# Two half loads of one row each in place of one load of two rows, for the gate rows of a head pair

## The chip, the cores and the metric

The kernel runs on one core of a Trainium2 chip. The metric is the device time of one execution in microseconds. Lower is better.

## The reference

The computation has three stages, all in float32, on 2 x 576 = 1152 tokens.

1. Causal attention with a forget gate, 2 batches x 8 heads, 576 positions, head size 64. `cum` is the running sum of log f along the positions:

```
scores = q @ k.T / 8
decay  = cum[:, None] - cum[None, :]
attn   = softmax(where(causal, scores + decay, -1e9))
x      = attn @ v            # heads side by side: 1152 x 512
```

2. A mixture of four experts, each weighted by a normalised probability p: `x = sum_e p[:, e] * (relu(x @ w1[e]) @ w2[e])`, with 512 x 1024 and 1024 x 512 weights.
3. A last block `out = (g(x @ w_in)) @ w_out` with g(h) = h * sigmoid(1.702 h) and 2048 hidden units.

Within a row of the softmax the term `cum[row]` is constant and falls out, so the kernel needs only a row vector for every head, `-cum[column]`, the same for all query rows. These vectors are the gate rows of the change.

## The kernel before, in words

Every matrix product of the experts is done as three products of rounded float32 parts (high x high, low x high, high x low), so each weight tile passes through a split: ScalarE or POOL writes the high part `whi` (lines 53 and 56), VectorE the low part `wlo` (line 173). Raw weights arrive by SP's queue in `wst`, four buffers; `load_pair` issues the next load when the split of an earlier one is done.

The attention runs while the first expert blocks are computed. `attention()` is a generator over units (one query tile of a head pair, or two tiles of one head). Each step emits stages of several units: the scores on TensorE (line 436), the maximum on VectorE (line 464), the exponential on ScalarE (line 480), the division by the sum on POOL (line 491), the transposes on TensorE (line 510), the copies `ph` on ScalarE, and the product with the values on TensorE (line 540). The main loop pulls steps of this generator between groups of expert matmuls (lines 639 and 683).

For each head pair of the later passes (eight in all) `load_heads` brings keys and queries (`kq`, `qr`), `prep_parts` and `prep_queries` split them on POOL (`khi`, `klo`, `qhi`, `qlo`), and `load_cum` brings the gate rows from the small DRAM tensor `cumd` (16 rows, one per head, 576 columns). It issues a tile `cb` for each of the two heads, one row broadcast to 128 partitions, and a tile `cbs` of 128 x 576 in which the first 64 partitions hold the row of the first head and the other 64 that of the second. `cbs` serves the last query tile, which has only 64 rows per head, so both heads share one 128-row tile. `prep_cum` then adds the causal triangle on POOL: to `cb` in lines 391 and 394, to the last 64 columns of `cbs` in line 397, once for each half. VectorE reads `cbs` in line 464. There are two `cbs` buffers.

All these loads are issued by `load` (line 62) on SP's queue, which works through its instructions in order; an instruction that must wait holds up all behind it. Tiles carry their dependences, and a planner that simulates the run (`schedule_with_timeline_sim`) writes down the order of each engine's instructions. Only the start (`start[0]`, `keep_in_program_order`) and a few steps (`pinned`) are fixed by hand. When the attention is done, `begin_late` frees its memory and `mlp_convert` starts to convert the last block's weights on VectorE (lines 222 to 238).

Of the kernel before, what the change touches and what calls it, by code (L numbers as in the profile page):

```python
# [15 lines left out]
B, H, S, D = 2, 8, 576, 64  # L16
# [19 lines left out]
def attn_moe_mlp(ctx: ExitStack, tc: tile.TileContext, qk0, qk1, qk2, v0, vp, fg, dp, wa_moe, wb_moe, wa_mlp, wb_mlp, outT):  # L36
# [8 lines left out]
    def pool(name, bufs, space=None, scope=ctx):  # L45
        kw = {} if space is None else {"space": space}
        return scope.enter_context(tc.tile_pool(name=name, bufs=bufs, **kw))
# [12 lines left out]
    def load(out, in_):  # L60

        ins = nc.sync.dma_start(out=out, in_=in_)
        if start[0]:
            tc.keep_in_program_order(ins)
# [37 lines left out]
    cumd = pool("cumd", 1, bass.MemoryType.DRAM).tile([16, S], F32, name="cumd")  # L102
# [271 lines left out]
    def load_cum(p, h0):  # L374

        cs, b, s0 = p
        st = pairs[p, h0]
        r = b * H + h0
        st["cb"] = [cb_p.tile([128, 896], F32, tag="cb", name="cb") for _ in range(2)]
        for g, cb in enumerate(st["cb"]):  # L380
            load(cb[:, :512], cumd[r + g:r + g + 1, :512].to_broadcast([128, 512]))
        st["cbs"] = cbs_p.tile([128, S], F32, tag="cbs", name="cbs")
        load(st["cbs"], cumd[r:r + 2, :].unsqueeze(1).to_broadcast([2, 64, S]))

    def prep_cum(p, h0):

# [172 lines left out]
    def attention():  # L559
# [21 lines left out]
        for i in range(len(seq) + L_X2 + 1):  # L581
# [3 lines left out]
            if i == 0:  # L585
                load_cum(*nxt[0])
# [3 lines left out]
            def prepare():  # L590
                for k in new:
                    prep_parts(*k)
                for k in new_q:
                    prep_queries(*k)
                for k in new:
                    load_cum(*k)
                    prep_cum(*k)
# [297 lines left out]
```

## Time and profile before

| what | value |
|---|---|
| time, median of 3 runs | 735.25 us (733.9 to 736.05) |
| the profiled execution | 733.54 us |
| its span, first to last instruction | 731.8 us |
| TensorE matmuls busy | 711.1 us, 97% |
| VectorE, POOL, ScalarE busy | 460.5, 291.0, 267.9 us |
| mean granted TensorE clock | 0.991 |
| moved by DMA | 68.83 MB, mean 94 GB/s |

All times inside the trace are microseconds from the start of the span. The time of an execution is a little longer than its span. Busy shares are averages over stages: the attention fills the first 225 us, the rest is expert and last-block matmuls.

### The profile page before, as it was taken

Reading aid. Unit: us, or ns where it says so; the run is one execution under the profiler, and the core shown is the slowest. Engines: PE = TensorE matmul, PEld = TensorE weight load, DVE = VectorE, ACT = ScalarE, POOL = GpSimd, SP = SyncE. Lnnn points to the kernel's source line nnn. Section 1 sums busy time; section 2 is a strip of 40 time slices with the busy share of each in tenths; the row PEclk is TensorE's granted clock in tenths of the full one; section 3 lists DMA queues with packets and bytes.
Section 4 is the critical chain, followed back from the end, with each engine's and each line's share of the span. In section 5 each row is a group of like instructions: output and inputs, shape, how many; then the busy total and the mean of one; then the engine's idle time right before and its main releaser. Section 6 shows DMA issues by size and latency. Waiting matters only on the chain.

```text
span 731.8 us, 12044 instructions
## 1 busy us (share of the span) xinstructions
PE 711.1 (97%) x4519; PEld 682.8 (93%) x4519; DVE 460.5 (63%) x1029; ACT 267.9 (37%) x630; POOL 291.0 (40%) x371
## 2 busy tenths in 40 slices
PE   7987989999999999999999999999999999999998
PEld 3776878898899999999998999999999999999997
DVE  5575737677758999999999542345962124424422
ACT  5354745576632233222221221223354433333320
POOL 6589787765422022332232432232462222222220
PEclk9899999999999999999999999999999999999999
DMA  8786643432225465453343210000100000000012
GB/s 261 226 251 219 175 159 127 134 101 67 81 88 195 144 203 161 144 189 116 115 144 116 87 30 29 1 1 1 58 1 0 1 1 1 1 1 0 1 44 87
DMA packets 31226, 68.83 MB, mean 94 GB/s; under 512 B 3224, under 2 KB 4768, under 8 KB 31168
## 3 DMA queue, kind: packets, MB, share of 16 engines
q1 hardware_dynamic: 31128, 68.02, 29.1%
q8 instruction: 36, 0.59, 0.3%
q14 instruction: 22, 0.18, 0.1%
q10 hardware_dynamic: 40, 0.04, 0.0%
HBM read 65.62 MB, written 2.41 MB: 93 GB/s over the span
## 4 chain that ended last, share of the span: by engine, by line
PE 69%; DVE 14%; DMA 6%; POOL 5%; issue 3%; ACT 1%; SPq 1%; DVEq 0%; ACTq 0%; POOLq 0%
PE m L683 32%; PE m L639 30%; PE s L436 3%; PE x L540 3%; DVE wlo L173 3%; DMA wst<-in_wa_moe_dram 2%; PE t L510 2%; DMA cbs<-cumd 2%; POOL e L491 2%; DVE cvd L236 1%; DVE hl L666 1%; DVE tmp L697 1%; DVE wf L230 1%; DVE cvt L224 1%; DMA mst<-in_wb_mlp_dram 1%
## 5 line engine op out<-in xcount | busy, mean ns | idle before, releaser
L699 POOL TENSOR_TENSOR acc<-acc,tmp 128x384 f32<-128x384 f32 (+3 forms) x112 | 111.7, 1009 | 237.3 <-DVE tmp L697 235.3
L683 PE MATMUL m<-hh,whi 128*128 128x384 f32 (+2 forms) x640 | 129.3, 321 | 0.2 <-DVE acc L694 0.2
L683 PE MATMUL m<-hh,wlo 128*128 128x384 f32 (+2 forms) x640 | 127.7, 320 | 1.2 <-DVE wlo L173 1.2
L683 PE MATMUL m<-hl,whi 128*128 128x384 f32 (+2 forms) x640 | 128.0, 319 | 0.0
L639 PE MATMUL m<-xh,wlo 128*128 128x384 f32 (+2 forms) x624 | 126.3, 320 | 0.0
L639 PE MATMUL m<-xl,whi 128*128 128x384 f32 (+2 forms) x624 | 126.2, 321 | 0.0
L639 PE MATMUL m<-xh,whi 128*128 128x384 f32 (+2 forms) x624 | 125.6, 321 | 0.0
L56 ACT ACTIVATE whi<-wst 128x512 fp32r<-128x512 f32 x104 | 65.3, 632 | 128.9 <-PE m L639 69.0
L173 DVE TENSOR_TENSOR wlo<-wst,whi 128x512 fp32r<-128x512 f32 x112 | 92.7, 830 | 24.6 <-ACT whi L56 18.2
L683 PEld LDWEIGHTS m<-hh,wlo 128*128 128x128 f32 x640 | 106.2, 189 | 1.9 <-DVE wlo L173 1.9
L683 PEld LDWEIGHTS m<-hh,whi 128*128 128x128 f32 x640 | 106.8, 190 | 0.6 <-DVE acc L694 0.4
L683 PEld LDWEIGHTS m<-hl,whi 128*128 128x128 f32 x640 | 106.4, 188 | 0.2
L639 PEld LDWEIGHTS m<-xh,wlo 128*128 128x128 f32 x624 | 104.1, 188 | 0.2
L639 PEld LDWEIGHTS m<-xl,whi 128*128 128x128 f32 x624 | 104.0, 188 | 0.2
L639 PEld LDWEIGHTS m<-xh,whi 128*128 128x128 f32 x624 | 103.7, 188 | 0.2
L674 POOL TENSOR_TENSOR hl<-tmp,hh 128x384 fp32r<-128x384 f32 x48 | 49.1, 1025 | 133.2 <-ACT hh L56 133.2
L665 ACT ACTIVATE hh<-m 128x384 fp32r<-128x384 f32 (+2 forms) x112 | 49.0, 437 | 114.4 <-PE m L639 114.0
L666 DVE SCALAR_TENSOR_TENSOR hl<-m,hh 128x384 fp32r<-128x384 f32 (+2 forms) x112 | 54.8, 492 | 32.5 <-ACT hh L665 32.5
L697 DVE TENSOR_TENSOR tmp<-m,dpb 128x384 f32<-128x384 f32 (+2 forms) x80 | 40.9, 512 | 33.3 <-PE m L683 26.8
L672 DVE TENSOR_TENSOR tmp<-m,sg 128x384 f32<-128x384 f32 x48 | 26.6, 554 | 54.5 <-ACT sg L671 52.7
L491 POOL TENSOR_SCALAR e<-e,sm 128x128 f32<-128x128 f32 (+4 forms) x72 | 46.5, 657 | 25.4 <-DVE sm L489 17.2
L480 ACT ACTIVATE e<-e,mx 128x128 f32<-128x128 f32 (+4 forms) x72 | 42.0, 583 | 33.3 <-DVE mx L464 29.2
(96 smaller groups left out, 774.8 us busy)
## 6 DMA issues: line engine op xcount, KB each, us to landing
wst<-in_wa_moe_dram SPq DMA_DIRECT2D x28, 512.0 KB, 3.7
wst<-in_wb_moe_dram SPq DMA_DIRECT2D x28, 512.0 KB, 3.8
mst<-in_wa_mlp_dram SPq DMA_DIRECT2D x16, 512.0 KB, 3.9
mst<-in_wb_mlp_dram SPq DMA_DIRECT2D x16, 512.0 KB, 3.7
cb<-cumd SPq DMA_DIRECT2D x16, 256.0 KB, 8.0
qr<-in_qk_dram SPq DMA_DIRECT2D x12, 256.0 KB, 9.4
kq<-in_qk_dram SPq DMA_DIRECT2D x8, 352.0 KB, 2.9
vd<-in_vp_dram SPq DMA_DIRECT2D x8, 320.0 KB, 8.2
```

Source lines behind the costliest of these rows:

```text
L56: return nc.scalar.activation(out=out, in_=in_, func=AF.Copy)
L173: sub = nc.vector.tensor_sub(lf, raw, f(hf))
L480: nc.scalar.activation(out=e[:, off:off + w], in_=e[:, off:off + w], func=AF.Exp, scale=-1.0, bias=mx, accum_out=sm[:, 0, k:k + 1])
L491: last_norm[:] = [nc.gpsimd.tensor_scalar(out=e[:, off:off + w], in0=e[:, off:off + w], scalar1=sm[:, 0, i:i + 1], scalar2=1.0, op0=ALU.mu ...
L639: nc.tensor.matmul(p[:, :n], lhsT=w[:, k, :], rhs=x[c][:, k, :], start=(j == 0 and k == 0), stop=(j == 2 and k == 3))
L665: nc.scalar.activation(out=hh[:, g, :n], in_=p[:, :n], func=AF.Relu)
L666: nc.vector.scalar_tensor_tensor(out=hl[:, g, :n], in0=p[:, :n], scalar=0.0, in1=f(hh[:, g, :n]), op0=ALU.max, op1=ALU.subtract)
L672: nc.vector.tensor_mul(t[:, :n], p[:, :n], s[:, :n])
L674: nc.gpsimd.tensor_sub(hl[:, g, :n], t[:, :n], f(hh[:, g, :n]))
L683: nc.tensor.matmul(p[:, :n], lhsT=w[:, k, :], rhs=x[:, k, :n], start=(j == 0 and k == 0), stop=(j == 2 and k == 3))
L697: nc.vector.tensor_mul(t[:, :n], p[:, :n], d)
L699: nc.gpsimd.tensor_add(a, a, t[:, z])
```

## The change

```diff
@@ -380,7 +380,8 @@
         for g, cb in enumerate(st["cb"]):
             load(cb[:, :512], cumd[r + g:r + g + 1, :512].to_broadcast([128, 512]))
         st["cbs"] = cbs_p.tile([128, S], F32, tag="cbs", name="cbs")
-        load(st["cbs"], cumd[r:r + 2, :].unsqueeze(1).to_broadcast([2, 64, S]))
+        for g in range(2):
+            load(st["cbs"][64 * g:64 * g + 64], cumd[r + g:r + g + 1, :].to_broadcast([64, S]))
 
     def prep_cum(p, h0):
 
```

Before, one load takes two rows of `cumd`, each repeated 64 times (a source of 2 x 64 x 576), and writes the 128 partitions of `cbs`. After, there are two loads: each takes one row, repeated 64 times, and writes 64 partitions. The bytes and the tile are the same.

## Rows read from the trace of the kernel before

**Rows 1.** Timeline of TensorE: start, us, what, idle time before it and releaser.
```profile
63.95 3.81 PE L540 MATMUL x<-ph,vd 128*64 128x320 f32 x16 [4.52 <-ACT ph L56]
...
92.36 0.65 PE L510 MATMUL t<-identr,e 128*128 128x128 f32 x4 [2.09 <-POOL e L491]
99.53 0.55 PE L510 MATMUL t<-identr,e 128*128 128x128 f32 x3 [0.78 <-POOL e L491]
105.09 0.66 PE L510 MATMUL t<-identr,e 128*128 128x128 f32 x4 [1.07 <-POOL e L491]
```

**Rows 2.** Busy time by stretch: length, PE, PEld, DVE, ACT, POOL, clock, DMA, GB/s.
```profile
63.95:67.10 3.15, 3.15 (x12) 2.78 (x14) 1.67 (x6) 2.64 (x9) 3.08 (x8) 0.51 0.35 111
```

**Rows 3.** Chain of waits, 30 to 85 us: start, us, what; the DMA pieces.
```profile
33.34 12.34 DMA cbs<-cumd
...
50.43 11.70 DMA wst<-in_wa_moe_dram
...
77.69 3.74 DMA cb<-cumd
```

**Rows 4.** Timeline of ScalarE around 62 us.
```profile
62.24 0.63 ACT L56 ACTIVATE whi<-wst 128x512 fp32r<-128x512 f32 x1 [4.78 <-DMA wst<-in_wa_moe_dram]
```

**Rows 5.** Timeline of VectorE around 49 us.
```profile
49.44 0.88 DVE L173 TENSOR_TENSOR wlo<-wst,whi 128x512 fp32r<-128x512 f32 x1 [1.56 <-POOL whi L53]
```

**Rows 6.** Timeline of POOL, 45 to 95 us.
```profile
45.75 0.70 POOL L397 TENSOR_TENSOR cbs<-cbs,tri 64x64 f32<-64x64 f32 x2 [3.25 <-DMA cbs<-cumd]
...
78.62 1.20 POOL L397 TENSOR_TENSOR cbs<-cbs,tri 64x64 f32<-64x64 f32 x2 [5.17 <-DMA cbs<-cumd]
79.89 1.71 POOL L363 TENSOR_TENSOR klo<-kq,khi 128x704 fp32r<-128x704 f32 x1
...
88.54 0.77 POOL L53 TENSOR_SCALAR khi<-kq 128x704 fp32r<-128x704 f32 x1
89.29 1.43 POOL L391 TENSOR_TENSOR cb<-cb,tri 128x384 f32<-128x384 f32 x1
...
94.61 0.71 POOL L397 TENSOR_TENSOR cbs<-cbs,tri 64x64 f32<-64x64 f32 x2 [2.30 <-DMA cbs<-cumd]
```

**Rows 7.** Waits over the run: who for whom, us in total, times, longest.
```profile
POOL cbs L397 <- DMA cbs<-cumd: 16.2, 6, 5.2
```

**Rows 8.** Waits of SP's queue over the run.
```profile
SPq L62 <- DMA cbs<-cumd: 5.9, 1, 5.9
...
SPq L202 <- PE t L510: 1.8, 1, 1.8
```

**Rows 9.** Timeline of SP's queue: issues of cbs loads.
```profile
70.18 0.51 SPq L62 DMA_DIRECT2D cbs<-cumd  x1
...
83.17 0.51 SPq L62 DMA_DIRECT2D cbs<-cumd  x1
```

**Rows 10.** Busy time by stretch, columns as in Rows 2.
```profile
75.00:76.00 1.00, 1.00 (x9) 0.96 (x9) 0.64 (x2) 1.00 (x4) 0.00 (x0) 1.00 0.13 51
78.00:79.00 1.00, 1.00 (x11) 1.00 (x10) 1.00 (x3) 1.00 (x3) 0.38 (x1) 1.00 1.01 391
```

**Rows 11.** DMA issues: count, KB each, median us from issue to landing.
```profile
wst<-in_wa_moe_dram SPq DMA_DIRECT2D x28, 512.0 KB, 3.7
...
kq<-in_qk_dram SPq DMA_DIRECT2D x8, 352.0 KB, 2.9
...
dpb<-dpT SPq DMA_DIRECT2D x2, 288.0 KB, 8.9
```

**Rows 12.** Issue durations on SP, ns min/median/max, first and last start (by tile).
```profile
L62 SPq DMA_DIRECT2D cbs<-cumd x8: 500/506/575, 14.1 to 154.9; - x8
...
L62 SPq DMA_DIRECT2D cb<-cumd x16: 326/360/976, 12.2 to 151.2; - x16
```

**Rows 13.** Busy time by stretch, columns as in Rows 2.
```profile
15.00:20.00 5.00, 3.99 (x12) 1.96 (x13) 4.02 (x17) 3.55 (x13) 1.36 (x2) 0.59 1.08 354
...
340.00:350.00 10.00, 10.00 (x60) 10.00 (x59) 10.00 (x19) 1.26 (x3) 3.75 (x3) 1.00 0.51 159
```

## The prediction

> **What bounds the kernel now.** I first read the busy table of the page: TensorE (PE) is busy for 711.1 of 731.8 us, so a change that touches no PE work can win only what PE loses to waits and to a low clock. The next view is the waits of PE in the order of time. After 64 us PE has four waits above 0.3 us: 4.52 us ahead of the value matmuls at 63.95 us, released by ScalarE, and 2.09, 0.78 and 1.07 us ahead of transposes between 92 and 106 us, all three released by POOL's normalisation of line 491 [rows 1]. From there to the end PE hardly waits, so a microsecond won in these places should reach the end. The first wait has a tail: from 63.95 to 67.10 us, just after PE stood idle, the granted clock is 0.51, the lower of the two levels (1.2 GHz), which costs 3.15 x 0.49 = 1.5 us [rows 2].
>
> Then I ask what ends last before these places. The chain of waits runs through three loads: the gate rows `cbs`, 12.34 us from 33.34 us on; a weight load `wst`, 11.70 us from 50.43 us on; and a `cb` load, 3.74 us [rows 3]. The weight load is the one behind the 4.52 us: ScalarE stands still for 4.78 us in front of the split of these weights at 62.24 us, and the copy that the value matmuls need is queued behind that split [rows 4]. It was issued late too, because VectorE's split, which frees the buffer, waited 1.56 us for POOL [rows 5], and POOL had stood still for 3.25 us before the `cbs` addition at 45.75 us. POOL does the same again for 5.17 us before 78.62 us and 2.30 us before 94.61 us [rows 6]; over the run it waits 16.2 us for these loads, in 6 places [rows 7]. SP also stands still for 5.9 us because of a `cbs` load [rows 8]. In the order of its issues that is the eighth load after the one of 33.34 us, which had to land first.
>
> Why is a load of 288 KB so slow? The SP queue issues two of them at 70.18 and 83.17 us [rows 9]; POOL sees them land at 78.62 and 94.61 us, after 8.4 and 11.4 us. While the first runs alone, at 75 to 76 us, the mean busy share of the 16 DMA engines is 0.13 at 51 GB/s; a `cb` load of 256 KB, a row broadcast to 128 partitions, brings the share to 1.01 and 391 GB/s at 78 to 79 us [rows 10]. 0.13 x 16 is 2.1: the transfer with two rows runs on two engines, one for each row, and the broadcast of one row on all of them. At 51 GB/s its 294,912 bytes alone take 5.8 us. Anything issued behind it (part of every load that is spread over 16 engines) waits on those two engines, which is the second reason for the 11.70 us of the weight load.
>
> **The change, part by part.** It removes eight loads that occupy two engines each and adds sixteen of 147,456 bytes, each with 64 as its first dimension; no compute instruction changes.
>
> *The new landing time.* The trace has no broadcast to 64 partitions. The nearest row is the `cb` load in the chain, with 3.74 us [rows 3]; the shortest of a like size is `kq` (352 KB) with 2.9 us and the longest the broadcast `dpb` (288 KB, in a crowded stretch) with 8.9 us [rows 11]. I take 3.7 us for a pair of halves and keep 2.9 and 8.9 as ends. With 3.7 us the load issued at 70.18 lands at 73.9; POOL was ready at 78.62 - 5.17 = 73.45, so 4.7 of its 5.17 us go. For the load of 83.17 all 2.30 go. The load of 33.34 may take 9.1 us before POOL (ready at 42.50) notices, more than the 8.9 of the worst row: all 3.25 go. So POOL is 3.25 us earlier by 46 us, 7.9 by 79 and 10.2 by 95.
>
> *The wait of 4.52 us and its clock.* ScalarE was ready for the weights at 62.24 - 4.78 = 57.46 us. With POOL 3.25 us earlier the weight load is issued at 47.2 instead of 50.43; with the typical 3.7 us of such a load [rows 11] it lands at 50.9, with its present 11.70 at 58.9, which would leave 1.4 us of the wait. Two blocked engines fewer speak for the first. I take the whole wait and its clock: 4.52 + 1.5 = 6.0 us (ends: 0 if the weights come late for another reason, 6.0).
>
> *What is late next.* Between 64 and 73 us POOL is only 3.25 us earlier while PE would be 6.0: PE can meet POOL's normalisations there and give back between 0 and 2.8 us. I take the middle, 1.4.
>
> *The waits for POOL at 92 to 106 us* sum to 3.94 us. POOL gains 10.2 us by then, PE 4.6, so POOL could cover all of it; but its inputs come from VectorE and ScalarE, which follow PE and get only PE's part. Ends 0 and 3.9; I take 2.0.
>
> *The added issues.* A `cbs` issue takes 506 ns on SP, a `cb` issue, the nearest for a half, 360 ns [rows 12]: 8 x (2 x 0.36 - 0.51) = 1.7 us more on SP in all, and one load more per head pair in a sequence in which the eighth load behind another waits for it. SP's own waits hide it. Without that cover it would be at most 0.2 us per pair on the load's way, 1.7 us in all.
>
> *The other waits on cbs* (16.2 - 3.25 - 5.17 - 2.30 = 5.5 us in three more places) have PE busy beside them; I count them at nothing, with 0.5 us as the upper end.
>
> Sum: 6.0 - 1.4 + 2.0 - 0 = 6.6 us. The profiled execution took 733.54 us (span 731.8), so 726.9 for its like. It was 1.7 us below the median of 735.25 us; against that median the forecast is 728.6 us. The terms' ends give from about 1 us slower (first term 0, issues 1.7, 0.5 won) to 10.4 us faster.
>
> One rule speaks against the change. The Trainium skill, page "DMA: Bandwidth & Descriptors", section "Rules for kernel authors", advises not to cut a transfer into two disjoint partition halves, since both halves use the same 16 engines and serialise. By that rule the time would stay at 735. The trace agrees only with half of its premise: the broadcast of one row does fill 16 engines (share 1.01), the one transfer that is cut here does not (0.13) [rows 10].
>
> **The rivals.**
> *Given back where VectorE is full.* From 230 to 400 us VectorE converts the later weights and is busy 10.00 of 10 us in a stretch such as 340 to 350 [rows 13]. If that work does not start earlier, PE arrives early and waits, and the time is 735.2. For it: the full VectorE. Against it: the load that starts the conversion is let go by PE's last transposes (SP waits 1.8 us for them) [rows 8], so it moves with PE.
> *The halves don't spread, or they serialise.* Then the loads stay near 8 us and nothing moves: 735. Against it stands the `cb` row at share 1.01; for it only that no load to 64 partitions is in the trace.
> *Slower: a new written order.* The order of every engine's instructions comes from a planner that simulates the loads. With two loads in place of one it can put a pair's preparation on POOL (klo 1.71, khi 0.77, cb 1.43 and what belongs to them, at least 3.9 us [rows 6]) ahead of a normalisation that PE's transposes wait for, between 80 and 106 us, where PE already follows POOL. Each pair placed so costs PE 3.9 us. One leaves 2.7 us of the gain; two cost 7.8 and turn it to 1.2 us slower, 736.5. So two pairs is the point from which it decides. For it: the order is not pinned in this stretch. Against it: the same data dependences and about the same bytes.
> *More than forecast.* If POOL's lead covers all of 3.94 us and PE gives nothing back, 9.9 us go; if the stretch at 15 to 20 us, where PE is busy 3.99 of 5 us at a clock of 0.59 [rows 13], also profits because the first `cbs` load no longer holds two engines, up to 13: 722 to 725.
>
> **How the numbers follow.** Forecast (2.3 to 9 us faster) 0.66; more than that 0.08; given back 0.09; no spreading 0.05; new order or another new wait with a loss 0.12. Below 0.3% (2.2 us), about what a measurement of this kernel tells from no change, lie the two neutral rivals: same 0.14. Faster 0.74, slower 0.12. The likeliest case alone spans 726 to 733. The range goes from 722, the larger gain, to 736.5, where the slower rival begins to win.
>
> **What would show it.** Right: the landing of `cbs` at 3 to 5 us and POOL's wait on it from 16.2 to below 2 us; the stretches with a DMA share of 0.13 gone; no wait of 5.9 us on SP; PE's wait of 4.52 us and the clock of 0.51 behind it gone; PE's waits on line 491 shorter. Wrong: halves that still take 8 us; the wait of 4.52 us in place although the loads are fast (then the weights were late for another reason); the order on POOL changed, with preparation ahead of normalisations; or a PE that arrives at 230 us early and at 405 us at the old time.

## The result, and the profile after

The changed kernel takes 725.45 us (median of 4, 721.94 to 726.55) against 735.39 us for the kernel before: ratio 0.9859, 95% interval 0.982 to 0.9899, so 9.9 us less. The forecast was 728.6 us with a range of 722 to 736.5. When the same kernel was timed again (e1 below), it took 725.87 us beside 734.13, 8.3 us less; so the gain is 8 to 10 us.

The waits of TensorE (PE) over the whole run, in total us, times and longest, are now these (lines behind the change have moved down by one):

```profile
PE s L437 <- DVE mx L465: 2.1, 3, 0.8
PE m L733 <- DVE acc L726: 1.9, 1, 1.9
PE t L511 <- POOL e L492: 1.6, 2, 1.4
PE m L684 <- DVE wlo L173: 1.3, 2, 0.7
```

The wait of 4.52 us for ScalarE ahead of the value matmuls [rows 1] is not among them, and of the waits for POOL's normalisation 1.6 us are left, all but 0.2 us of it in the first 30 us. The timelines of TensorE, ScalarE and POOL show the places that answer to [rows 1, 4, 6]: no bracket with an idle time stands behind any of them. One fence for each engine:

```profile
56.71 2.16 PE L541 MATMUL x<-ph,vd 128*64 128x320 f32 x16
```

```profile
56.14 0.62 ACT L56 ACTIVATE whi<-wst 128x512 fp32r<-128x512 f32 x1
```

```profile
40.20 1.15 POOL L398 TENSOR_TENSOR cbs<-cbs,tri 64x64 f32<-64x64 f32 x2
...
68.48 1.49 POOL L398 TENSOR_TENSOR cbs<-cbs,tri 64x64 f32<-64x64 f32 x2
...
82.51 0.70 POOL L398 TENSOR_TENSOR cbs<-cbs,tri 64x64 f32<-64x64 f32 x2
```

Sixteen value matmuls take 2.16 us where they took 3.81 at the low clock [rows 1, 2]. POOL's 16.2 us of waiting for `cbs` [rows 7] have no line in the list of waits any more, and neither has SP's wait of 5.9 us behind such a load [rows 8]. By tile, the loads look like this (issue duration in ns min/median/max; landing in us min/median/max):

```profile
L62 SPq DMA_DIRECT2D cbs<-cumd x16: 450/460/794, 14.0 to 141.9; - x16
...
DMA to landing us min/median/max: 2.9/4.8/7.2
```

The DMA engines while the halves issued at 119.61 us run alone, by stretch (length, PE, PEld, DVE, ACT, POOL, clock, DMA share, GB/s):

```profile
121.00:122.00 1.00, 1.00 (x10) 1.00 (x9) 0.89 (x2) 0.57 (x3) 1.00 (x2) 1.00 0.49 184
```

The share is 0.49 at 184 GB/s where the old load left it at 0.13 and 51 [rows 10]. That is the work of about eight engines, not of 16, so the share alone does not say how many carry a half. The trace shows it in another way: it keeps the moments at which a load reports its landing. The reports go with the engines: two for a `cbs` load before, at a share of 0.13; four in e3 below, at 0.25; eight for each half in e10, at 0.52; 16 for each half in the changed kernel. (A load with fewer than 16 has one more about 1 us after its issue, before its first packet moves: 71.13 against 72.25 us for the load of 70.18. It is left out.)

**Where the time went.** The first 30 us vary by some 4 us from execution to execution of one and the same kernel: the second `cbs` load is issued at 31.06 us in the profile above, at 35.48 us in a second profile of the same kernel. So I compare stretches between two marks that every kernel has on SP's queue: the issue of the second `cbs` load (near 33 us) and the first `mst` load, which opens the last block when the attention is done. After:

```profile
31.06 1.09 SPq L62 DMA_DIRECT2D cbs<-cumd  x2
...
206.08 0.82 SPq L202 DMA_DIRECT2D mst<-in_wa_mlp_dram  x2
```

and before, where the first mark is the one of 33.34 us [rows 3]:

```profile
218.37 0.82 SPq L202 DMA_DIRECT2D mst<-in_wa_mlp_dram  x2
```

Of the 11.6 us between the two spans (731.8 and 720.2), 2.3 are the start (33.34 to 31.06) and vary; 10.0 are the stretch between the marks (185.0 to 175.0); the rest of the run is 0.7 us longer (513.4 to 514.1). So the gain is made between 33 and 218 us. The second profile gives 175.2 for the stretch and 514.9 us for the rest, so 0.7 to 1.5 us of the gain are missing again after the second mark.

The two traces, set side by side, give the gain by place. Counted by the columns that TensorE has streamed since the first mark, the changed kernel is ahead of the kernel before by 6.4 us when that one stands at 68 us, by 5.4 at 92, by 9.1 at 106 and by 10.0 from 170 us on; at 400 us it is 9.3. In the second profile the same places give 5.6, 5.0, 9.0, 9.9 and 8.3.

The planner did write a new order: SP's queue differs only in single places, but POOL's, ScalarE's, VectorE's and TensorE's differ from about 50 us on until the attention ends. Hence the question for the experiments: did the engines of the load make the gain, or the new order, or the two pieces?

### The profile page after: what moved, and what is told of

Its sections match the earlier page's. It is cut to its first block, busy times and chain, and to the rows that moved or that the text cites. A ratio compares the mean times of both kernels' runs of the same rounds, so it can differ in the third digit from the quotient of the medians.

```text
span 720.2 us, 12063 instructions
## 1 busy us (share of the span) xinstructions
PE 709.6 (99%) x4519; PEld 680.4 (94%) x4519; DVE 458.9 (64%) x1029; ACT 269.0 (37%) x630; POOL 295.2 (41%) x371
## 4 chain that ended last, share of the span: by engine, by line
PE 86%; DVE 6%; POOL 4%; issue 2%; DMA 1%; ACT 0%; SPq 0%; POOLq 0%; DVEq 0%
PE m L684 38%; PE m L640 37%; PE s L437 3%; PE x L541 3%; PE t L511 3%; DVE wlo L173 1%; POOL e L492 1%; POOL acc L700 1%; POOL qlo L372 1%; DMA qr<-in_qk_dram 1%; DVE tmp L698 1%; PE m L661 1%; DVE e L465 1%; DVE cvd L236 1%; DVE hl L667 1%
## 5 line engine op out<-in xcount | busy, mean ns | idle before, releaser
L640 PE MATMUL m<-xh,whi 128*128 128x384 f32 (+2 forms) x624 | 127.1, 322 | 0.0
L173 DVE TENSOR_TENSOR wlo<-wst,whi 128x512 fp32r<-128x512 f32 x112 | 92.8, 832 | 21.7 <-ACT whi L56 16.6
```

The source lines that it names most:

```text
L173: sub = nc.vector.tensor_sub(lf, raw, f(hf))
L640: nc.tensor.matmul(p[:, :n], lhsT=w[:, k, :], rhs=x[c][:, k, :], start=(j == 0 and k == 0), stop=(j == 2 and k == 3))
```

## The experiments

Each was timed in 5 rounds beside the kernel before. The last column is the stretch between the two marks in the run's profile. The numbers of engines are those of the reports in its trace: 2, 4, 8 and 16 for each `cbs` load.

| run | loads per pair, engines, order | time, us | ratio to before (95%) | stretch, us |
|---|---|---|---|---|
| before | 1, on 2, its own | 734.1 to 735.4 | 1 | 185.0 |
| e1_after_again | 2, on 16, after | 725.87 | 0.988 (0.985 to 0.991) | 175.2 |
| e2_two_on_two_engines | 2, on 2, after | 740.74 | 1.009 (1.006 to 1.012) | 190.3 |
| e9_two_on_four_engines | 2, on 4, after | 726.75 | 0.988 (0.985 to 0.991) | 175.5 |
| e10_two_on_eight_engines | 2, on 8, after | 726.06 | 0.987 (0.985 to 0.990) | 175.5 |
| e11_four_loads | 4, on 16, mixed | 725.21 | 0.986 (0.984 to 0.989) | 175.7 |
| e4_one_on_16_engines | 1, on 16, a third | 728.30 | 0.992 (0.990 to 0.995) | 177.2 |
| e3_one_on_four_engines | 1, on 4, before | 726.98 | 0.991 (0.988 to 0.994) | 175.8 |
| e5_stored_twice_two_engines | 1, on 2, before | 734.78 | 1.001 (0.999 to 1.002) | 185.0 |
| e6_second_pair_only | second pair's on 4 | 732.10 | 0.996 (0.995 to 0.998) | 180.6 |
| e7_third_pair_only | third pair's on 4 | 732.67 | 0.997 (0.995 to 0.998) | 182.5 |
| e8_fourth_pair_and_later | from the fourth pair on 4 | 730.55 | 0.994 (0.993 to 0.996) | 180.8 |

**Engines against order and number.** The changed kernel again:

> The changed kernel once more, beside the others. Every theory: 725.5 us, 0.986 of the time before.

Measured 725.87 us. Then the same two loads, with the same written order on every engine, confined to two engines by the shape of the source alone:

```diff
-            load(st["cbs"][64 * g:64 * g + 64], cumd[r + g:r + g + 1, :].to_broadcast([64, S]))
+            load(st["cbs"][64 * g:64 * g + 64], cumd[r + g:r + g + 1, :].unsqueeze(1).to_broadcast([2, 32, S]))
```

> Two loads per pair, as in the changed kernel, but each row is repeated as 2 x 32 rather than 64 times, so that each load should run on two engines again. The written order of every engine's instructions is that of the changed kernel. Theory spread (the gain comes from the 16 engines): landing back at 8 us or more, POOL waits for cbs over 10 us in all, DMA shares of 0.13 are back, and the time is 733 to 737 us. Rival order (the planner's new order makes the gain): 724 to 727 us. Rival two loads (two semaphores, smaller pieces): 724 to 727 us.

Measured 740.74 us: above the 733 to 737 us expected and slower even than the kernel before. While such a load runs alone, the DMA share falls to two engines again,

```profile
138.00:139.00 1.00, 1.00 (x11) 1.00 (x10) 1.00 (x1) 0.95 (x5) 1.00 (x2) 1.00 0.13 30
```

and POOL waits longer for `cbs` than ever, now for each half by itself (waits, then POOL's timeline):

```profile
POOL cbs L398 <- DMA cbs<-cumd: 23.5, 10, 3.5
```

```profile
80.32 0.32 POOL L398 TENSOR_TENSOR cbs<-cbs,tri 64x64 f32<-64x64 f32 x1 [2.76 <-DMA cbs<-cumd]
83.71 0.32 POOL L398 TENSOR_TENSOR cbs<-cbs,tri 64x64 f32<-64x64 f32 x1 [3.08 <-DMA cbs<-cumd]
```

So neither the new order nor the cut into two makes the gain; both rivals fall. With everything else fixed, the engines are worth 14.9 us.

The opposite corner: one load and the old order, on four engines. Each row of `cumd` is stored twice, so that a pair has four source rows.

```diff
-        load(st["cbs"], cumd[r:r + 2, :].unsqueeze(1).to_broadcast([2, 64, S]))
+        load(st["cbs"], cumd[2 * r:2 * r + 4, :].unsqueeze(1).to_broadcast([4, 32, S]))
...
-    nc.scalar.dma_start(out=cumd, in_=fr)
+    nc.scalar.dma_start(out=cumd.rearrange("(r k) s -> r k s", k=2), in_=fr.unsqueeze(1).to_broadcast([16, 2, S]))
```

> The kernel before with each row of cumd stored twice, so that the one load per pair reads 4 x 32 rows and should run on four engines. The order of the instructions stays that of the kernel before, but for five lines on POOL. Theory spread: 73.7 KB per engine in place of 147 KB, some 2.9 us in place of 5.8, landing near 5.5 us, POOL's waits on cbs from 16.2 to about 4 us, time 727 to 731 us. Rivals order and two loads: no change, 734 to 736 us.

Measured 726.98 us, at the lower edge of what was expected, with POOL's wait at 2.4 us. While the load runs alone the DMA share is 0.25, four engines:

```profile
128.00:129.00 1.00, 1.00 (x11) 1.00 (x10) 1.00 (x6) 0.15 (x2) 1.00 (x2) 1.00 0.25 97
```

The wait of TensorE for ScalarE is gone in this run too; ScalarE's own wait in front of the split of the weights is 1.16 us where it was 4.78 [rows 4]:

```profile
57.50 0.63 ACT L56 ACTIVATE whi<-wst 128x512 fp32r<-128x512 f32 x1 [1.16 <-DMA wst<-in_wa_moe_dram]
```

The same idea with each row stored eight times:

```diff
-        load(st["cbs"], cumd[2 * r:2 * r + 4, :].unsqueeze(1).to_broadcast([4, 32, S]))
+        load(st["cbs"], cumd[8 * r:8 * r + 16, :].unsqueeze(1).to_broadcast([16, 8, S]))
...
-    nc.scalar.dma_start(out=cumd.rearrange("(r k) s -> r k s", k=2), in_=fr.unsqueeze(1).to_broadcast([16, 2, S]))
+    nc.scalar.dma_start(out=cumd.rearrange("(r k) s -> r k s", k=8), in_=fr.unsqueeze(1).to_broadcast([16, 8, S]))
```

> The kernel before with each row of cumd stored eight times (288 KB written at the start in place of 36 KB), so that the one load per pair reads 16 x 8 rows and should run on 16 engines. The planner writes an order of its own for it. Theory spread: POOL's waits on cbs below 2 us, time 723 to 728 us. Rival two loads: 734 to 737 us. The order theory says nothing firm, since the order is a third one.

Measured 728.30 us, just outside the upper end; POOL no longer waits for `cbs`, as expected. The planner's order is a third one and 288 KB are written at the start, so I don't read the difference to 727 us; one load on 16 engines does win, which the rival of two loads denied.

**How many engines.** Two loads and the order of after, on four and on eight engines:

```diff
-            load(st["cbs"][64 * g:64 * g + 64], cumd[r + g:r + g + 1, :].to_broadcast([64, S]))
+            load(st["cbs"][64 * g:64 * g + 64], cumd[r + g:r + g + 1, :].unsqueeze(1).to_broadcast([4, 16, S]))
```

(`[8, 8, S]` for eight).

> As the run with two loads on two engines, same order of all instructions, but each row is repeated as 4 x 16, so that each load should run on four engines: 73.7 KB per engine and pair, 2.9 us at 25 GB/s. Theory spread with a threshold (what counts is that the load lands before POOL wants it): 726 to 729 us, nearly all of the 15 us between two and sixteen engines. Rival proportional (the time that engines are held counts byte by byte): a bit over half of it, 731 to 734 us.

> The same on eight engines, 36.9 KB per engine and pair. Threshold: 725 to 727 us. Proportional: 728 to 730 us.

740.74, 726.75, 726.06 and 725.87 us on 2, 4, 8 and 16 engines: a threshold, not a proportion, within what these medians can tell. POOL's waits on `cbs` are 23.5, 4.2, 1.0 and 1.0 us in these four. Once the load lands in time, more speed buys nothing here. More pieces cost nothing that can be measured either:

```diff
-        for g in range(2):
-            load(st["cbs"][64 * g:64 * g + 64], cumd[r + g:r + g + 1, :].to_broadcast([64, S]))
+        for g in range(4):
+            load(st["cbs"][32 * g:32 * g + 32], cumd[r + g // 2:r + g // 2 + 1, :].to_broadcast([32, S]))
```

> Four loads of 32 partitions per pair, each row broadcast, all on 16 engines; the planner changes part of the order on VectorE, ScalarE and POOL, none on TensorE. If an added load costs only its issue on SP, hidden as I counted it: 725 to 727 us. Rival (with eight loads behind each other allowed, more loads per pair hold SP up): POOL waits for cbs again, 728 us or more.

Measured 725.21 us, within the spread of the changed kernel.

**Which load is worth what.** The next four share one order of instructions, that of e3, and differ only in which pairs read `[4, 32, S]`; the others read `[2, 64, S]` out of the same doubled storage:

```diff
+        two = cumd.rearrange("(r k) s -> r k s", k=2)[r:r + 2, 0, :].unsqueeze(1).to_broadcast([2, 64, S])
-        load(st["cbs"], cumd[2 * r:2 * r + 4, :].unsqueeze(1).to_broadcast([4, 32, S]))
+        load(st["cbs"], cumd[2 * r:2 * r + 4, :].unsqueeze(1).to_broadcast([4, 32, S]) if r == 2 else two)
```

(never, `r == 2`, `r == 4`, `r >= 6`).

> Control for the next three: each row of cumd is stored twice, but every cbs load still reads 2 x 64 rows, on two engines. The order of all instructions is that of the kernel on four engines and, but for five lines on POOL, of the kernel before. Every theory: the time before, 733 to 736 us. If storing twice had itself been the gain: 727.

Measured 734.78 us: storing twice costs nothing that can be measured, and the control holds.

> As the control, but the load of the second pair (the one POOL waits for at 45.75 us) runs on four engines. Theory 'POOL and SP waited for this load': POOL is 3 us earlier, the weight load behind it is issued earlier, the PE wait of 4.5 us at 64 us shrinks: 3 to 6 us faster than the control. Rival 'the weights are late because the next cbs load (third pair) sits on two of their engines': the weight load still lands late, under 2 us faster.

Measured 2.7 us less than the control, 4.4 us less in the stretch: between the 3 us at which the first theory began and the 2 us at which the rival ended. The chain of waits shows why it is not the whole of the first term:

```profile
48.39 11.71 DMA wst<-in_wa_moe_dram
```

The weight load is issued at 48.39 us, 13.8 us after the first mark (16.6 in the control), so 2.8 us earlier, as the prediction reasoned; but the chain still gives it 11.71 us. The reports say where these go: the split waits for the first of three weight loads that are issued in a row here, and of its 16 engines fourteen have reported by 53.64 us, the last two only at 58.71 and 60.10, just after the third pair's `cbs` load, still on two engines, has reported at 56.86 and 58.24. The kernel before has the same picture: fourteen by 55.71 us, the last two at 60.80 and 62.13, and the third pair's load at 58.96 and 60.29. So the rival is right about this part: the weights wait for the two engines of the load ahead of them. PE's wait shrinks from 4.74 us in the control to 2.95, and the clock behind it is still the low level (timeline, then busy time by stretch):

```profile
61.92 1.07 PE L541 MATMUL x<-ph,vd 128*64 128x320 f32 x2 [2.95 <-ACT ph L56]
```

```profile
61.92:65.00 3.08, 3.08 (x12) 2.71 (x14) 1.59 (x6) 2.64 (x9) 3.08 (x7) 0.50 0.37 107
```

> As the control, but only the load of the third pair (issued 2.4 us ahead of the late weight load) runs on four engines. POOL never waited for that one. Theory 'POOL and SP waited for the second pair's load': within 1.5 us of the control. Rival 'engines held in front of the weights': the weight load lands in 6 to 8 us instead of 11.7, 3 to 5 us faster.

Measured 2.1 us less than the control. POOL still waits 2.13 us for the second pair's load, but the weight load lands in 10.49 us and PE waits 2.03 us. Neither theory forecast both: a fast load of the third pair alone takes 2.7 us off the wait of 4.74 us that the control has at this place, a fast load of the second pair alone 1.8 us, and only with both is it gone (e3, after). Landing in 10.49 us is short of the 6 to 8 us that the rival asked for. The reports show why. Twelve engines have finished their part of the weights by 56.99 us, four only at 58.41 to 60.85, the third pair's load at 55.83 to 58.99. That load comes so late because the second pair's load, still on two engines, has held up what stands behind it: a key load issued at 38.19 us has fourteen reports by 44.63 us and the last two at 49.65 and 50.29. That these two are among the four is inferred, since a report does not name its engine. With both loads spread, the same weight load lands 5.8 us after its issue at 44.66 us in the changed kernel, 4.8 us in the second profile, with no group of late engines. From the trace by tile, for the issue at 44.66 us:

```profile
DMA to landing us min/median/max: 5.8/5.8/5.8
```

Not all of what e7 wins here lasts. By the streamed columns PE is 4.2 us ahead of the control at 80 us and 2.4 at 92: it meets POOL's normalisations, as the prediction's term for what is given back says, though later than that term had it, and waits for them longer than the control does. The longest of these waits:

```profile
91.54 0.66 PE L511 MATMUL t<-identr,e 128*128 128x128 f32 x4 [1.73 <-POOL e L492]
```

Behind e7's shorter wait the clock stays high:

```profile
62.67 2.43 PE L541 MATMUL x<-ph,vd 128*64 128x320 f32 x16 [2.03 <-ACT ph L56]
```

```profile
62.67:65.00 2.33, 2.33 (x16) 1.23 (x16) 0.99 (x4) 2.33 (x9) 2.16 (x6) 1.00 0.92 311
```

> As the control, but the loads of the fourth to eighth pair run on four engines. They can only touch POOL's waits from 78 us on (5.17, 2.30 us and the smaller ones) and PE's three waits for POOL of 3.94 us. My sum has 2.0 us for it; 1 to 4 us faster than the control. If the gains of the three parts add up, they give the 7 us of the kernel with all loads on four engines; if each wait only uncovers the next one, their sum is less.

Measured 4.2 us less than the control, 4.2 in the stretch too. The wait of 4.51 us ahead of the value matmuls is untouched; the wait for POOL near 90 us falls from 2.09 to 0.44:

```profile
63.57 3.76 PE L541 MATMUL x<-ph,vd 128*64 128x320 f32 x16 [4.51 <-ACT ph L56]
90.27 0.66 PE L511 MATMUL t<-identr,e 128*128 128x128 f32 x4 [0.44 <-POOL e L492]
```

By the streamed columns 3.2 us of e8's gain are won between 80 and 106 us, 0.4 later, and 0.6 before its first fast load is issued; that last part is not its doing.

The three parts sum to 2.7 + 2.1 + 4.2 = 9.0 us, the whole is 734.78 - 726.98 = 7.8 us: they nearly add up. By stretches 4.4 + 2.5 + 4.2 = 11.1 against 9.2.

No version beats the changed kernel by more than the spread: 725.21 to 726.98 us are one result.

## Why the prediction was right, point by point

**Two engines.** Shown. The share in the trace read as 2.1 engines was the mechanism: 2 x 32 rows bring 0.13 back, 4 x 32 rows make it 0.25, and the reports count 2, 4, 8 and 16 engines. The Trainium skill, page "DMA: Bandwidth & Descriptors", section "Rules for kernel authors", says that an outermost dimension of size c below 16 confines a DMA to at most c engines; the traces agree for 2, 4 and 8. The Trainium skill's rule against cutting a transfer into halves, in the same section and weighed in the prediction, gives as its reason that both halves use all 16 engines anyway; the single transfer here used two. e2, e3 and e11 show that spreading decides, and that on 16 engines four pieces cost nothing measurable over two.

**Landing.** 3.7 us was taken with ends of 2.9 and 8.9; the profile after shows 2.9 to 7.2 with a median of 4.8. A bit more than taken, but in time: POOL waits for none of them.

**The wait of 4.52 us and its clock, 6.0 us less 1.4 given back.** The wait and the low clock behind it are gone in the profile after. Both reasons that the prediction gave for the late weights were at work. POOL's earlier start issues the weight load 2.8 us earlier (e6; the prediction had 3.25). The two held engines, its second reason, are the rest: the reports put the last two parts of the weights right behind the third pair's load (e6 and the kernel before). What was off is the landing: 3.7 us taken, 5.8 and 4.8 measured, which was still early enough. Neither e6 nor e7 alone brings it below 10 us. By the streamed columns the term measured 6.4 us (5.6 in the second profile), and 1.0 (0.6) of it was gone again by 92 us, without a wait of PE that would show why, so 5.4 (5.0) were left for the 4.6 of the sum.

**The waits for POOL at 92 to 106 us, 2.0 us.** This is the mis-sized term. I had reasoned that POOL's inputs follow PE and took the middle of 0 and 3.9. All three waits are gone in the profile after, and PE wins 3.7 us (4.0 in the second profile) between 92 and 106 us. With PE's first wait still in place (e8) it wins 3.2 us there of the 3.6 us of waits that the control has.

**The other waits on `cbs`, counted at nothing.** From 106 to 170 us PE wins another 0.9 us in both profiles, where the sum had 0 and 0.5 as its upper end.

**Where that leaves the size.** The 9.9 us of the result lie beyond the 9 us at which the likeliest case ended, in the rival "more than forecast", which had a chance of 0.08; the 8.3 us of the repetition lie within the likeliest case. The first condition of that rival, that POOL's lead covers all of the 3.94 us, is what happened. Whether its second holds, that PE gives nothing back, is open, since PE's loss between 80 and 92 us comes without a wait. The start, its third, varies too much between two profiles of one kernel to be judged.

**The added issues.** Hidden, as said: 16 loads of 460 ns in place of 8 of 506 ns, 3.3 us more on SP where I had 1.7, and even 32 loads cost nothing in e11.

**The rivals.** Given back where VectorE is full: in small part. The run after the second mark takes 514.1 and 514.9 us in the two profiles of the changed kernel, 513.4 before and 512.8 to 516.0 over all versions. In the second profile PE waits 0.54 us for VectorE at 361.88 us, which it does not do before. The prediction had counted four waits of PE above 0.3 us after 64 us; it missed 0.62 and 0.60 us at 397.22 and 402.25, both for VectorE, which the change leaves in place. A new written order: it did come, and it can have done harm only with late loads. With two loads on two engines it is 5.3 us slower in the stretch than the kernel before (190.3 and 185.0); with four engines or more the two orders are alike (175.5 and 175.8). Whether the order or the cut into two makes those 5.3 us is open: no run has one of them without the other on two engines.

## What to carry to other kernels

Read the mean DMA share while a load runs alone: a value like 0.13 says that it sits on two of sixteen engines, and here that cost 8 to 10 us of 735 although the waits that named it stood on POOL and SP and not on the engine that bounds the kernel. Make sure that it does run alone: what other loads have left on the same engines looks the same. And look at what is issued behind it: a load spread over all engines is complete only when its last part is, and here that part stood behind the narrow load. Look at the outermost dimension of the source, and give it enough rows or cut the load; past the point where it lands before its reader is ready, more engines or more pieces changed nothing measurable here. An edit to a load can rewrite the order of all engines, so an experiment that keeps the order and changes only the shape of the source is worth more than a comparison of two free orders.

## What the runs showed of the hardware that was not expected

Behind a wait of TensorE of 2.95 us the granted clock was 0.50 for the next 3.08 us, behind one of 2.03 us at the same place of the same order it was 1.00 (e6 and e7). These are one profile each, and the length of the wait alone does not decide it: in the profile after, the mean granted clock from 41 to 45 us is 0.57, at least in part the lower of the two levels, behind waits of at most 0.81 us.

A weight load of 512 KB issued behind the two-engine load was complete on fourteen engines 5.3 us after its issue and on the last two after 10.4 and 11.7 us (the kernel before, load issued at 50.43 us).
